# Theta's products in float32 on the transposed x, and x in DRAM by pairs of batches

## The chip, the cores and the metric

The kernel runs on one NeuronCore of a Trainium2 chip. Its engines are TensorE (PE in the profile, PEld for its weight loads), VectorE (DVE), ScalarE (ACT), GpSimd (POOL) and SyncE (SP, which issues the DMAs). The metric is the device time of one execution in microseconds (us).

## The reference

Three layers run one after the other on B = 4 batches of S = 768 positions with DM = 320 channels (8 heads of 40). The first is a gated linear attention; its output, laid out as x[b, s, 320], feeds the second layer, which is the one that the change touches:

```
theta = x @ w_theta
zr = x * cos(theta);  zi = x * sin(theta)
y = einsum('ts,bsd->btd', w_tok_r, zr) + einsum('ts,bsd->btd', w_tok_i, zi)
u = x + y
x2 = u + max(u @ w_ch, 0)
```

The third layer takes x2: a convolution of 5 taps over positions with a sigmoid gives a gate, and the output is (gate * (x2 @ w_val)) @ w_out. All of it is float32.

## The kernel before

The program is written as a list of steps, and a planner sets the order. Each call on `pe`, `act`, `dve`, `pool`, `sp` (or on a choice of two, such as `any2`, DVE or POOL) is recorded by `Unit.record` (line 67 of the profile is that helper, so nearly all instructions carry L67). `Plan.order` then runs a list schedule: each step has a cost from `Plan.cost`, a due time that comes from PE's order, and the free engine that can take it first gets it; a step with two possible engines gets the slower one only while its due time allows. `Plan.issue` repeats this four times and keeps the order with the earliest planned end. A change to one part can so move instructions everywhere, and move steps between DVE and POOL.

The work has two stages. In the first, `attend(d)` runs attention over 12 groups (a batch and a pair of 128-position chunks each). `finish(g)` scales the group's output in a tile `x_m` (two 640-column multiplications, on DVE or POOL), and `store_x(g)` writes it to the DRAM tile `x_dr`, laid out [batch, position, 320], with two DMAs. Between groups `cv_piece` turns a third of a weight matrix from 64-bit into float32, and for theta's weights into a rounded high part `th_hi` and a low part `th_lo`.

In the second stage `theta(p, c)` runs 12 times, for two pairs of batches p and six chunks c of 128 positions (steps 1 to 6 are p = 0, steps 7 to 12 are p = 1). One step reads x of both batches into a tile `x_m` with two DMAs, transposes it on PE in five blocks of 128 columns (the fifth holds the last 64 channels of both batches), and copies it out of PSUM twice: with ACT into the tile `xT_m`, which is u's place later on, and as a rounded high part and a low part into `xh_m` (ACT copies, DVE subtracts, lines 797 to 807). PE then forms theta for each batch out of eight products of 320 columns: high by high, high by low and low by high for two blocks, and two products for the last block. ACT rounds theta to a whole number of turns (`th_m`), DVE subtracts, ACT takes the sine and cosine, and for both parts x is multiplied in and the result split into high and low (`z`; 640 columns each, on DVE or POOL).

`weight(p, th_i, c)` prepares the token weights of a step: DVE works on the bits of a 64-bit tile (`r_b`) and subtracts to get the low part (`wt_m`); for the second pair they are read back from DRAM (`w_r`). `mix` multiplies z by them, 30 products of 384 columns per step, into five PSUM banks. Between the mixes the functions `f_u`, `f_ch`, `f_val` and `f_out` do the rest of the layers: `f_u` adds the mix's result into `xT_m`, then come products with `ch`, the convolution on DVE, products with `val` and with `out`. Within the planned order every engine works strictly in its own row, and semaphores join them.

Of the kernel before, what the change touches and what calls it, by code (L numbers as in the profile page):

```python
# [7 lines left out]
F32 = mybir.dt.float32  # L8
F32R = mybir.dt.float32r
# [3 lines left out]
AF = mybir.ActivationFunctionType  # L13
ALU = mybir.AluOpType
# [3 lines left out]
B, H, S, D = 4, 8, 768, 40  # L18
DM = H * D
L = 128  # L20
# [52 lines left out]
class Plan:  # L73
# [47 lines left out]
    def cost(self, unit, op, out, ins):  # L121

        n = self.elems(out, 1)
        if unit == "pe":
            if op == "transpose":
                return 0.11
            m, kind = ins[0].shape[-1], ins[0].dtype
            if kind == F32R:
                return (n + 32) / 2400
            rows = 2 if ins[0].shape[0] <= 64 else 1  # L130
            tiles = rows * (2 if m <= 64 else 1)
            if kind == BF16:
                return max((n + 6) / 2400, 0.05) / tiles
            return 2 * max((2 * n + 10) / 2400, (m + 6) / 1200) / tiles
        if unit == "act":
            return n / 1200 + (0.051 if ins[0].space == PSUM else 0.093) + 0.093 * (len(ins) > 1)
        if unit == "pool":
            if op == "tensor_tensor":
                wide = all(st or c == 1 for a in ins for st, c in list(a.ap)[1:])
                return n * (0.0021 if wide else 0.00166) + 0.15  # L140
            return n / 1200 + {"affine_select": 0.2, "tensor_copy": 0.17, "copy": 0.17}.get(op, 0.035)
        if unit == "sp":
            return self.DMA_ISSUE
        fast = op in ("tensor_scalar", "tensor_copy", "copy") and all(a.space != PSUM for a in [out] + ins)
        each = 0.06 * any(self.elems(a, 1) == 1 < n for a in ins)
        return n * (6 if op == "reciprocal" else 1) / (1920 if fast else 960) + 0.068 + each
# [195 lines left out]
def tile_kernel(ctx, tc, qT, kT, kt, v1, og, ig, fg, w_th, w_ch, w_val, w_out, cw, wtok,  # L342
# [17 lines left out]
    def words(n, name, dtype=F32, place=None, bufs=1):  # L360

        t = sb.tile([128, n], dtype, name=name, tag=place or name, bufs=bufs)
        k = turn(place, bufs) if place else 0
        plan.place[t.name] = f"{place or name}.{k}"
        return t
# [3 lines left out]
    halfpi, magic = words(1, "halfpi"), words(1, "magic")  # L369
    dve.memset(halfpi, HALFPI)  # L370
    dve.memset(magic, MAGIC)
    x_dr = dr.tile([B, S, DM], F32, name="x_dr")
    wt_dr = dr.tile([2, NC, 128, 4 * TH], F32, name="wt_dr")


    wsp = {}
    for nm, n, m in (("th", DM, DM), ("ch", 384, 256), ("val", 384, 256), ("out", DM, DM)):
        wsp[nm] = [words(3 * c, f"{nm}_{s}", F32R).rearrange("p (k n) -> p k n", k=3)
                   for s, c in (("hi", n), ("lo", m))]

# [80 lines left out]
    def half(i):  # L461
        return slice(64 * i, 64 * i + 64)
# [134 lines left out]
    def store_x(g):  # L597
        b, g3 = divmod(g, NC // GC)
        so = st.pop(("so", g)).rearrange("p (u d) -> p u d", u=2)
        for i in range(2):  # L600
            t0 = (g3 * GC + i) * L
            sp.dma_start(out=x_dr[b, t0:t0 + L, :].rearrange("(u p) d -> p u d", p=U), in_=so[half(i)])


    def cv_piece(nm, src, k_):
        t = turn("cv", 2)
        raw = xT_m[1][:, t * 2 * DM:(t + 1) * 2 * DM].bitcast(I64)
        v = xT_m[1][:, (4 + t) * DM:(5 + t) * DM]
        if nm == "cw":
            raw, v = raw[:, 0:15], cw_sb.rearrange("p j t -> p (j t)")  # L610
        sp.dma_start(out=raw, in_=src if nm == "cw" else src[:, k_ * DM:(k_ + 1) * DM])
        cv_abs(raw, v)
        cv_bits(raw, v)
        if nm == "cw":
            return
        if nm == "th":
            dve.tensor_scalar(out=v, in0=v, scalar1=INV2PI, scalar2=None, op0=ALU.mult)
        hi, lo = wsp[nm]
        act.activation(out=hi[:, k_, 0:DM], in_=v, func=AF.Copy)
        n = DM if nm in ("th", "out") else 256  # L620
        any2.tensor_tensor(out=lo[:, k_], in0=v[:, 0:n], in1=hi[:, k_, 0:n].bitcast(F32),
                           op=ALU.subtract)
        if n < DM:
            any2.tensor_tensor(out=hi[:, k_, DM:384], in0=v[:, 256:DM],
                               in1=hi[:, k_, 256:DM].bitcast(F32), op=ALU.subtract)
# [126 lines left out]
            store_x(d)  # L752


    xh_m = words(20 * L, "xh_m", F32R, place="xh").rearrange("p (j l) -> p j l", l=L)
    wt_m = [words(4 * TH, f"wt_m{i}", F32R, place=f"w{i}").rearrange("p (s r t) -> p s r t", s=2, r=2)
            for i in range(2)]
    hl_f = words(8 * TH, "hl_f", F32R, place="q").rearrange("p (s j t) -> p s j t", s=2, j=4)
# [7 lines left out]


    def blk(x, j):
        return x[:, j * 128:(j + 1) * 128]

    def passes(out, prods):
        with plan.joined():
            for n, (l, r) in enumerate(prods):
                pe.matmul(out, l, r, start=n == 0, stop=n == len(prods) - 1)

    def split_rest(src, sr, eng):

        act.activation(out=sr[0:64, 0], in_=src[0:64], func=AF.Copy)
        act.activation(out=sr[64:128, 1], in_=src[64:128], func=AF.Copy)
        eng.tensor_tensor(out=sr[64:128, 0], in0=src[0:64], in1=sr[0:64, 0].bitcast(F32),  # L780
                          op=ALU.subtract)
        eng.tensor_tensor(out=sr[0:64, 1], in0=src[64:128], in1=sr[64:128, 1].bitcast(F32),
                          op=ALU.subtract)

    def ps_tile():
        return bank[turn("s", 2)] if stage[0] == 0 else (
# [2 lines left out]

    def theta(p, c):  # L790
        x = x_m[turn("x", XB)]
        src = x_dr[2 * p:2 * p + 2, c * L:(c + 1) * L, :].rearrange("b t d -> t b d")
        sp.dma_start(out=x[:, 0:512].rearrange("t (b d) -> t b d", b=2), in_=src[:, :, 0:256])
        sp.dma_start(out=x[:, 512:640].rearrange("t (b d) -> t b d", b=2), in_=src[:, :, 256:DM])
        xT = st["xT", p, c // 3] = xT_m[c // 3].rearrange("p (j t) -> p j t", j=5)
        o = slice((c % 3) * L, (c % 3) * L + L)
        xm = xh_m[:, 10 * (c % 2):10 * (c % 2 + 1)]
        xh, xl, xr = xm[:, 0:4], xm[:, 4:8], xm[:, 8:10]
        tps = ps_tile().rearrange("p (j l) -> p j l", j=4)
        with plan.joined():  # L800
            for j in range(4):
                pe.transpose(tps[:, j, :], blk(x, j), id_sb)
        tp4 = ps_tile()[:, 0:L]
        pe.transpose(tp4, blk(x, 4), id_sb)
        act.activation(out=xh, in_=tps, func=AF.Copy)
        dve.tensor_tensor(out=xl, in0=tps, in1=xh.bitcast(F32), op=ALU.subtract)
        split_rest(tp4, xr, dve)
        act.activation(out=xT[:, 0:4, o], in_=tps, func=AF.Copy)
        act.activation(out=xT[:, 4, o], in_=tp4, func=AF.Copy)
        wh, wl = wsp["th"]  # L810
        fr, rn = th_m[:, 0:2 * DM], th_m[:, 2 * DM:3 * DM]
        sc = th_m[:, 3 * DM:7 * DM].rearrange("p (r d) -> p r d", r=2)
        for bb in range(2):
            th = ps_tile()[:, 0:DM]
            pr = []
            for k_ in range(2):
                j = 2 * bb + k_
                pr += [(xh[:, j], wh[:, k_]), (xh[:, j], wl[:, k_]), (xl[:, j], wh[:, k_])]
            passes(th, pr + [(xr[:, bb], wh[:, 2]), (xr[:, bb], wl[:, 2])])

            act.activation(out=rn, in_=th, func=AF.Identity, bias=magic)
            for a, n, o in ((0, 256, 256 * bb), (256, 64, 512 + 64 * bb)):
                dve.scalar_tensor_tensor(out=fr[:, o:o + n], in0=rn[:, a:a + n], scalar=MAGIC,
                                         in1=th[:, a:a + n], op0=ALU.subtract, op1=ALU.subtract)
        z_hi, z_lo = (words(4 * DM, "z", F32R, place="z", bufs=2 * NC)
                      .rearrange("p (r d) -> p r d", r=2) for _ in range(2))
        with plan.joined():
            act.activation(out=sc[:, 1], in_=fr, func=AF.Sin, scale=-TWOPI)
            act.activation(out=fr, in_=fr, func=AF.Abs)
            act.activation(out=sc[:, 0], in_=fr, func=AF.Sin, scale=-TWOPI, bias=halfpi)  # L830
        for ri in (1, 0):
            any2.tensor_tensor(out=sc[:, ri], in0=sc[:, ri], in1=x, op=ALU.mult)
            act.activation(out=z_hi[:, ri], in_=sc[:, ri], func=AF.Copy)
            any2.tensor_tensor(out=z_lo[:, ri], in0=sc[:, ri], in1=z_hi[:, ri].bitcast(F32),
                               op=ALU.subtract)
        st["z", p, c] = (z_hi, z_lo)
# [289 lines left out]
```

## Time and profile before

| | |
|---|---|
| time, median of 3 runs | 427.25 us (426.7 to 428.12) |
| the profiled execution's own time | 428.13 us |
| its span, first to last instruction | 426.4 us |
| mean granted clock of TensorE | 0.872 of full speed |
| attention | up to about 125 us |
| theta steps 1 to 6, first mixes | 125 to 208 us |
| first fused part (`f_u` to `f_val`) beside mixes | 208 to 250 us |
| theta steps 7 to 12 beside mixes, `out`, `ch` | 250 to 322 us |
| the rest | 322 to 426.4 us |

The profile comes from one execution. Its span is 1.7 us shorter than that execution's time, since the start and the end of the program lie outside it. Busy time of an engine is the time in which at least one of its instructions runs; instructions of one engine overlap a little, so the mean of one instruction is somewhat longer than the distance between two. A row of the timeline ends with the idle time of the engine just before it and with what ended that idle time.

### The profile page before, as it was taken

How to read it: one execution, taken by the hardware profiler on the slowest of the kernel's cores; microseconds unless marked ns; L12 is line 12 of the kernel's file. 1: busy time of each engine (PE TensorE's matmuls, PEld its weight loads, DVE VectorE, ACT ScalarE, POOL GpSimd, SP SyncE). 2: the span in 40 equal slices, each digit the busy share in tenths (PEclk: the TensorE clock that was granted, in tenths of full speed). 3: DMA queues.
4: the chain of work that ended last, by engine and by line, in shares of the span. 5: the costliest groups of instructions: out<-in, count | busy, mean ns of one | idle time of the engine just before them, and what ended most of it. 6: DMA issues, size and time to landing. Idle time of an engine off the chain costs nothing.

```text
span 426.4 us, 11793 instructions
## 1 busy us (share of the span) xinstructions
PE 369.0 (87%) x4876; PEld 348.0 (82%) x4876; DVE 341.8 (80%) x714; ACT 224.6 (53%) x393; POOL 92.4 (22%) x103
## 2 busy tenths in 40 slices
PE   5686994896977595898999969999999999999985
PEld 4575884786876484798899959999999999999974
DVE  7875788499788689899999996758998449667993
ACT  2660515335126987777545366766578324134634
POOL 1212436142345333200011032005100002011600
PEclk9577568568587579889999989999999999999999
DMA  6986769768787553955856128620221530000202
GB/s 179 248 237 168 229 185 233 209 206 237 219 230 220 168 189 106 302 191 180 317 174 234 47 85 277 234 90 34 74 82 67 180 118 20 0 2 1 78 15 92
DMA packets 32373, 65.64 MB, mean 154 GB/s; under 512 B 6752, under 2 KB 19200, under 8 KB 32320
## 3 DMA queue, kind: packets, MB, share of 16 engines
q1 hardware_dynamic: 32320, 64.90, 48.9%
q8 instruction: 38, 0.62, 0.7%
q14 instruction: 15, 0.12, 0.1%
HBM read 47.58 MB, written 17.30 MB: 152 GB/s over the span
## 4 chain that ended last, share of the span: by engine, by line
PE 50%; DVE 30%; issue 8%; ACT 8%; DMA 2%; SPq 1%; ACTq 0%; DVEq 0%
PE bank L67 50%; DVE k_m L67 10%; DVE th_m L67 3%; DVE r_b L67 3%; DVE z L67 2%; DVE xh_m L67 2%; ACT th_m L67 2%; DVE xT_m L67 1%; ACT xT_m L67 1%; SPq L67 1%; DMA r_b<-in_kt_dram 1%; DVE f_m L67 1%; DMA r_b<-in_wtok_dram 1%; ACT xh_m L67 1%; DVE wt_m L67 1%
## 5 line engine op out<-in xcount | busy, mean ns | idle before, releaser
L67 PE MATMUL bank<-wt_m,z 128*128 128x384 f32 x480 | 88.6, 341 | 2.1 <-DVE th_m L67 1.0
L67 PEld LDWEIGHTS bank<-wt_m,z 128*128 128x128 f32 x480 | 84.5, 191 | 3.0 <-ACT z L67 1.7
L67 DVE SCALAR_TENSOR_TENSOR k_m<-k_m,cw_sb,k_m 128x384 f32<-128x384 f32 x76 | 46.4, 660 | 0.3
L67 PE MATMUL bank<-th_hi,xh_m 128*128 128x320 f32 x120 | 34.8, 364 | 12.4 <-DVE xh_m L67 7.9
L67 PE MATMUL bank<-w_r,z 128*128 128x384 f32 x240 | 43.7, 337 | 0.0
L67 PEld LDWEIGHTS bank<-w_r,z 128*128 128x128 f32 x240 | 41.5, 188 | 0.0
L67 ACT ACTIVATE W<-bank 128x512 f32<-128x512 f32 x24 | 14.2, 596 | 46.4 <-PE bank L67 45.6
L67 PEld LDWEIGHTS bank<-th_hi,xh_m 128*128 128x128 f32 x120 | 24.8, 227 | 15.1 <-DVE xh_m L67 9.3
L67 PE MATMUL bank<-q_m,k_m 40*64 40x64 f32 x768 | 21.2, 274 | 12.7 <-issue 8.4
L67 PEld LDWEIGHTS bank<-q_m,k_m 40*64 40x64 f32 x768 | 19.0, 185 | 13.5 <-issue 9.0
L67 ACT ACT_TABLE_LOAD x19 | 24.4, 1283 | 1.9 <-DVE W L67 1.6
L67 DVE TENSOR_TENSOR W<-W,bank 128x512 f32<-128x512 f32 x24 | 15.5, 676 | 12.3 <-PE bank L67 12.2
L67 PE MATMUL bank<-th_lo,xh_m 128*128 128x320 f32 x72 | 24.9, 347 | 0.0
L67 DVE SCALAR_TENSOR_TENSOR r_b<-r_b,r_b 128x768 int32<-128x768 int32 x24 | 23.9, 999 | 0.2
L67 DVE TENSOR_TENSOR k_m<-k_m,bank 104x164 f32<-104x164 f32 (+1 forms) x36 | 14.9, 421 | 10.1 <-PE bank L67 7.0
L67 PE MATMUL bank<-r_b,kw_m 64*40 64x41 f32 x704 | 19.1, 250 | 3.8 <-issue 2.5
L67 ACT ACTIVATE f_m<-bank 64x384 f32<-64x384 f32 x16 | 7.8, 486 | 27.3 <-PE bank L67 26.0
L67 PE MATMUL bank<-r_b,W 64*64 64x41 f32 x768 | 20.4, 272 | 1.4 <-issue 1.4
L67 ACT ACTIVATE th_m<-th_m 128x640 f32<-128x640 f32 (+1 forms) x27 | 18.9, 702 | 5.0 <-DVE th_m L67 3.1
L67 DVE TENSOR_TENSOR xh_m<-bank,xh_m 64x128 fp32r<-64x128 f32 (+1 forms) x36 | 15.2, 422 | 7.3 <-ACT xT_m L67 4.8
L67 PEld LDWEIGHTS bank<-r_b,W 64*64 64x64 f32 x768 | 18.5, 184 | 2.9 <-issue 2.8
L67 PEld LDWEIGHTS bank<-r_b,kw_m 64*40 64x40 f32 x704 | 15.9, 159 | 6.0 <-issue 3.1
(172 smaller groups left out, 936.3 us busy)
## 6 DMA issues: line engine op xcount, KB each, us to landing
r_b<-in_wtok_dram SPq DMA_DIRECT2D x24, 384.0 KB
wt_dr<-wt_m SPq DMA_DIRECT2D x12, 768.0 KB
w_r<-wt_dr SPq DMA_DIRECT2D x8, 768.0 KB
r_b<-in_v_dram SPq DMA_DIRECT2D x12, 328.0 KB
q_m<-in_qT_dram SPq DMA_DIRECT2D x24, 160.0 KB
k_m<-in_kT_dram SPq DMA_DIRECT2D x24, 160.0 KB
r_b<-in_kt_dram SPq DMA_DIRECT2D x12, 320.0 KB
x_m<-in_og_dram SPq DMA_DIRECT2D x24, 160.0 KB
```

Source lines behind the costliest of these rows:

```text
L67: calls[u] = lambda e=e: getattr(e, op)(*args, **kw)
```

## The change

Theta's weights are no longer split. `cv_piece` scales the float32 weights into a tile `w_t[0]`, and ACT copies them into a second one, `w_t[1]`, whose columns are in another order (the last 64 first). Theta's products take the transposed x in `xT_m` and these weights as float32: three products per batch, two with 128 rows and one with the 64 rows of the last block. `xh_m`, its copies and subtractions and the helper `split_rest` are gone. In DRAM x now lies by pairs of batches: [pair, position, 640], the first batch's 320 channels, then the second batch's last 64, then its first 256. So the middle 128 columns are the block that both batches share, a step reads x with one DMA, and the rounded theta is subtracted with one instruction of 320 columns instead of two. `store_x` needs two DMAs for each half of an odd batch. In `Plan.cost` a wide float32 product no longer counts as sharing the array.

```diff
@@ Plan.cost
             tiles = rows * (2 if m <= 64 else 1)
+            if kind == F32 and n > U:
+                tiles = 1
@@ tiles
-    x_dr = dr.tile([B, S, DM], F32, name="x_dr")
+    x_dr = dr.tile([B // 2, S, 2 * DM], F32, name="x_dr")
+    w_t = [words(3 * DM, f"w_t{bb}").rearrange("p (k n) -> p k n", k=3) for bb in range(2)]
-    for nm, n, m in (("th", DM, DM), ("ch", 384, 256), ("val", 384, 256), ("out", DM, DM)):
+    for nm, n, m in (("ch", 384, 256), ("val", 384, 256), ("out", DM, DM)):
@@ store_x
-            sp.dma_start(out=x_dr[b, t0:t0 + L, :].rearrange("(u p) d -> p u d", p=U), in_=so[half(i)])
+            to = x_dr[b // 2, t0:t0 + L].rearrange("(u p) d -> p u d", p=U)
+            if b % 2 == 0:
+                sp.dma_start(out=to[:, :, 0:DM], in_=so[half(i)])
+            else:
+                sp.dma_start(out=to[:, :, 384:], in_=so[half(i), :, 0:256])
+                sp.dma_start(out=to[:, :, DM:384], in_=so[half(i), :, 256:DM])
@@ cv_piece
         if nm == "th":
-            dve.tensor_scalar(out=v, in0=v, scalar1=INV2PI, scalar2=None, op0=ALU.mult)
+            w0, w1 = (t[:, k_] for t in w_t)
+            dve.tensor_scalar(out=w0, in0=v, scalar1=INV2PI, scalar2=None, op0=ALU.mult)
+            act.activation(out=w1[:, 64:], in_=w0[:, 0:256], func=AF.Copy)
+            act.activation(out=w1[:, 0:64], in_=w0[:, 256:], func=AF.Copy)
+            return
@@ blk
-        return x[:, j * 128:(j + 1) * 128]
+        o = (0, 1, 3, 4, 2)[j] * 128
+        return x[:, o:o + 128]
@@ theta
-        src = x_dr[2 * p:2 * p + 2, c * L:(c + 1) * L, :].rearrange("b t d -> t b d")
-        sp.dma_start(out=x[:, 0:512].rearrange("t (b d) -> t b d", b=2), in_=src[:, :, 0:256])
-        sp.dma_start(out=x[:, 512:640].rearrange("t (b d) -> t b d", b=2), in_=src[:, :, 256:DM])
+        sp.dma_start(out=x, in_=x_dr[p, c * L:(c + 1) * L])
...
-        act.activation(out=xh, in_=tps, func=AF.Copy)
-        dve.tensor_tensor(out=xl, in0=tps, in1=xh.bitcast(F32), op=ALU.subtract)
-        split_rest(tp4, xr, dve)
         act.activation(out=xT[:, 0:4, o], in_=tps, func=AF.Copy)
         act.activation(out=xT[:, 4, o], in_=tp4, func=AF.Copy)
...
-                pr += [(xh[:, j], wh[:, k_]), (xh[:, j], wl[:, k_]), (xl[:, j], wh[:, k_])]
-            passes(th, pr + [(xr[:, bb], wh[:, 2]), (xr[:, bb], wl[:, 2])])
+            r = slice(64 * bb, 64 * bb + 64)
+            passes(th, [(xT[:, 2 * bb + k_, o], w_t[bb][:, k_]) for k_ in range(2)]
+                   + [(xT[r, 4, o], w_t[bb][r, 2])])
             act.activation(out=rn, in_=th, func=AF.Identity, bias=magic)
-            for a, n, o in ((0, 256, 256 * bb), (256, 64, 512 + 64 * bb)):
-                dve.scalar_tensor_tensor(out=fr[:, o:o + n], in0=rn[:, a:a + n], scalar=MAGIC,
-                                         in1=th[:, a:a + n], op0=ALU.subtract, op1=ALU.subtract)
+            dve.scalar_tensor_tensor(out=fr[:, bb * DM:(bb + 1) * DM], in0=rn, scalar=MAGIC, in1=th,
+                                     op0=ALU.subtract, op1=ALU.subtract)
```

The planner makes a new order out of this, for all engines. Counted over the whole program, DVE has 716 instructions before and 675 now, ACT 395 and 361, POOL 108 and 86; SP has 240 of them both times. Two places of the order follow; in it `bank_106` and the like are PSUM banks, a name with a number is one of several equal tiles, and "x3" is a row that repeats.

On PE, behind the last products with `val` of the first fused part, where step 7 begins, there stood before:

```order
L67 MATMUL bank_108<-sr_f,val_hi 128x384
L67 MATMUL bank_106<-id_sb,x_m_82 128x128 x4
L67 MATMUL bank_107<-id_sb,x_m_82 128x128
L67 MATMUL bank_108<-th_hi,xh_m 128x320
L67 MATMUL bank_108<-th_lo,xh_m 128x320
L67 MATMUL bank_108<-th_hi,xh_m 128x320 x2
L67 MATMUL bank_108<-th_lo,xh_m 128x320
```

and there stands now (`id_sb` with `x_m` are the transposes, `wt_m` with `z` the mix):

```order
L67 MATMUL bank_108<-sr_f,val_hi 128x384
L67 MATMUL bank_106<-id_sb,x_m_82 128x128 x4
L67 MATMUL bank_107<-id_sb,x_m_82 128x128
L67 MATMUL bank_101<-wt_m_109,z 128x384 x6
L67 MATMUL bank_108<-w_t_71,xT_m_90 128x320 x3
L67 MATMUL bank_106<-w_t_72,xT_m_90 128x320 x3
L67 MATMUL bank_102<-wt_m_109,z 128x384 x6
```

The first six of the 30 products of a mix moved in between the transposes and theta's products, of which there are six in place of sixteen.

On POOL, at the end of attention and in theta steps 1 to 6, there stood before (`x_m` by `num_m` is attention's last scaling, `z` and `th_m` are theta's):

```order
L67 MEMSET k_m_87 128x5x4
L67 TENSOR_TENSOR z<-th_m,z 128x640 x2
L67 TENSOR_TENSOR x_m_79<-x_m_79,num_m 128x640
L67 TENSOR_TENSOR val_lo<-xT_m_91,val_hi 128x256
L67 TENSOR_TENSOR val_hi<-xT_m_91,val_hi 128x64
L67 TENSOR_TENSOR out_lo<-xT_m_91,out_hi 128x320
L67 TENSOR_TENSOR x_m_80<-x_m_80,num_m 128x640
L67 TENSOR_TENSOR th_m<-th_m,x_m_82 128x640
```

and there stands now:

```order
L67 MEMSET k_m_87 128x5x4
L67 TENSOR_TENSOR wt_m_109<-r_b_86,wt_m_109 128x768
L67 TENSOR_TENSOR val_lo<-xT_m_91,val_hi 128x256 x2
L67 TENSOR_TENSOR hl_f<-xT_m_90,hl_f 128x768
L67 TENSOR_TENSOR hl_f<-k_m_87,hl_f 128x768
L67 COPY halo<-k_m_87 128x20
```

The `z`, `th_m` and `x_m` instructions of this stretch are in DVE's row now; in the whole program POOL keeps two of theta's 640-column instructions (eight before) and three of attention's (eight before).

## Rows read from the trace of the kernel before

**Rows 1.** The page: busy time, share of the span and instructions by engine.

```profile
PE 369.0 (87%) x4876; PEld 348.0 (82%) x4876; DVE 341.8 (80%) x714; ACT 224.6 (53%) x393; POOL 92.4 (22%) x103
```

**Rows 2.** Windows: start:end, length, busy by engine (instructions), clock, DMA share, GB/s.

```profile
125.00:208.00 83.00, 65.24 (x637) 59.94 (x637) 72.67 (x148) 61.85 (x106) 18.34 (x15) 0.84 0.63 201
208.00:250.00 42.00, 40.51 (x235) 39.97 (x233) 41.06 (x72) 20.07 (x29) 5.72 (x4) 1.00 0.44 161
250.00:322.00 72.00, 68.75 (x412) 67.44 (x412) 59.08 (x112) 49.40 (x92) 12.71 (x8) 0.98 0.42 140
```

**Rows 3.** Chain that ended last: start us, length us, what it ran through.

```profile
252.84 38.75 PE bank L67 x231
...
322.16 67.27 PE bank L67 x393
```

**Rows 4.** Groups: count, busy us, mean ns, idle before; last row: ns min/median/max, first and last start.

```profile
L67 DVE TENSOR_TENSOR xh_m<-bank,xh_m 64x128 fp32r<-64x128 f32 (+1 forms) x36 | 15.2, 422 | 7.3 <-ACT xT_m L67 4.8 <-ACT xh_m L67 1.9
...
L67 ACT ACTIVATE xh_m<-bank 64x128 fp32r<-64x128 f32 (+1 forms) x36 | 12.2, 373 | 5.6 <-DVE num_m L67 4.7 <-PE bank L67 0.7
...
L67 DVE SCALAR_TENSOR_TENSOR th_m<-th_m,bank 128x256 f32<-128x256 f32 x24 | 10.0, 418 | 1.9 <-ACT th_m L67 1.5
...
L67 DVE SCALAR_TENSOR_TENSOR th_m<-th_m,bank 128x64 f32<-128x64 f32 x24 | 5.1, 214 | 0.0
...
L67 DVE SCALAR_TENSOR_TENSOR th_m<-th_m,bank x48: 209/314/422, 134.5 to 320.0; 128x256 f32<-128x256 f32 x24, 128x64 f32<-128x64 f32 x24
```

**Rows 5.** Groups: 640-column instructions of theta and attention, by engine.

```profile
L67 DVE TENSOR_TENSOR z<-th_m,z 128x640 fp32r<-128x640 f32 x21 | 16.6, 818 | 0.1
...
L67 POOL TENSOR_TENSOR x_m<-x_m,num_m 128x640 f32<-128x640 f32 x8 | 11.2, 1397 | 14.2 <-DVE num_m L67 4.3 <-DVE x_m L67 3.7 <-DMA k_m<-in_selG_dram 3.5
...
L67 POOL TENSOR_TENSOR th_m<-th_m,x_m 128x640 f32<-128x640 f32 x5 | 8.4, 1678 | 23.9 <-ACT th_m L67 23.9
...
L67 POOL TENSOR_TENSOR z<-th_m,z 128x640 fp32r<-128x640 f32 x3 | 5.2, 1755 | 18.6 <-ACT z L67 18.6
```

**Rows 6.** Timeline of DVE: first and last of five waits for x parts behind 134.5.

```profile
149.57 1.33 DVE L67 TENSOR_TENSOR xh_m<-bank,xh_m 128x512 fp32r<-128x512 f32 x3 [0.42 <-ACT xT_m L67]
...
194.05 1.01 DVE L67 TENSOR_TENSOR xh_m<-bank,xh_m 128x512 fp32r<-128x512 f32 x2 [0.80 <-ACT xT_m L67]
```

**Rows 7.** Timeline of PE: eight products of step 3, the transposes behind, warm-up; its window.

```profile
158.23 0.32 PE L67 MATMUL bank<-th_hi,xh_m 128*128 128x320 f32 x1
...
159.41 0.71 PE L67 MATMUL bank<-id_sb,x_m 128*128 128x128 f32 x5
...
2.08 5.68 PE L67 MATMUL bank<-num_m 128*128 128x256 f32 x14 [2.08 <-DVE halfpi L67]
...
4.00:6.00 2.00, 2.00 (x6) 1.64 (x5) 1.97 (x6) 0.00 (x0) 0.29 (x1) 1.00 0.53 161
```

**Rows 8.** Timeline of PE at step 7: transposes, first products, the rest, the mix.

```profile
247.80 0.71 PE L67 MATMUL bank<-id_sb,x_m 128*128 128x128 f32 x5
250.13 0.38 PE L67 MATMUL bank<-th_hi,xh_m 128*128 128x320 f32 x1 [1.62 <-DVE f_m L67]
...
252.84 0.90 PE L67 MATMUL bank<-th_hi,xh_m 128*128 128x320 f32 x2 [2.18 <-DVE xh_m L67]
...
256.47 5.37 PE L67 MATMUL bank<-wt_m,z 128*128 128x384 f32 x30
```

**Rows 9.** Waits, first and second half: who for whom, us, times, longest.

```profile
PE bank L67 <- DVE xh_m L67: 5.1, 4, 1.7
...
PE bank L67 <- DVE xh_m L67: 2.8, 2, 2.2
```

**Rows 10.** DMAs of x on SP (ns, first and last start), transposes of step 1.

```profile
L67 SPq DMA_DIRECT2D x_dr<-x_m x24: 575/602/1971, 43.5 to 170.0; - x24
L67 SPq DMA_DIRECT2D x_m<-x_dr x24: 365/422/597, 117.4 to 265.1; - x24
...
127.09 1.33 PE L67 MATMUL bank<-id_sb,x_m 128*128 128x128 f32 x5
```

More of the change, by code (lines that the diff above doesn't have):

```diff
@@ L616, in cv_piece @@
         if nm == "th":
-            dve.tensor_scalar(out=v, in0=v, scalar1=INV2PI, scalar2=None, op0=ALU.mult)
+            w0, w1 = (t[:, k_] for t in w_t)
[3 more added lines that the diff above has]
+            return
         hi, lo = wsp[nm]
         act.activation(out=hi[:, k_, 0:DM], in_=v, func=AF.Copy)
-        n = DM if nm in ("th", "out") else 256
+        n = DM if nm == "out" else 256
         any2.tensor_tensor(out=lo[:, k_], in0=v[:, 0:n], in1=hi[:, k_, 0:n].bitcast(F32),
@@ L752, in attend @@
             store_x(d)
-    xh_m = words(20 * L, "xh_m", F32R, place="xh").rearrange("p (j l) -> p j l", l=L)
     wt_m = [words(4 * TH, f"wt_m{i}", F32R, place=f"w{i}").rearrange("p (s r t) -> p s r t", s=2, r=2)
@@ L774, in passes @@
                 pe.matmul(out, l, r, start=n == 0, stop=n == len(prods) - 1)
[L776 to L783, printed above, removed]
     def ps_tile():
@@ L791, in theta @@
         x = x_m[turn("x", XB)]
-        src = x_dr[2 * p:2 * p + 2, c * L:(c + 1) * L, :].rearrange("b t d -> t b d")
-        sp.dma_start(out=x[:, 0:512].rearrange("t (b d) -> t b d", b=2), in_=src[:, :, 0:256])
-        sp.dma_start(out=x[:, 512:640].rearrange("t (b d) -> t b d", b=2), in_=src[:, :, 256:DM])
+        sp.dma_start(out=x, in_=x_dr[p, c * L:(c + 1) * L])
         xT = st["xT", p, c // 3] = xT_m[c // 3].rearrange("p (j t) -> p j t", j=5)
         o = slice((c % 3) * L, (c % 3) * L + L)
-        xm = xh_m[:, 10 * (c % 2):10 * (c % 2 + 1)]
-        xh, xl, xr = xm[:, 0:4], xm[:, 4:8], xm[:, 8:10]
         tps = ps_tile().rearrange("p (j l) -> p j l", j=4)
@@ L804, in theta @@
         pe.transpose(tp4, blk(x, 4), id_sb)
-        act.activation(out=xh, in_=tps, func=AF.Copy)
-        dve.tensor_tensor(out=xl, in0=tps, in1=xh.bitcast(F32), op=ALU.subtract)
-        split_rest(tp4, xr, dve)
         act.activation(out=xT[:, 0:4, o], in_=tps, func=AF.Copy)
         act.activation(out=xT[:, 4, o], in_=tp4, func=AF.Copy)
-        wh, wl = wsp["th"]
         fr, rn = th_m[:, 0:2 * DM], th_m[:, 2 * DM:3 * DM]
@@ L814, in theta @@
             th = ps_tile()[:, 0:DM]
-            pr = []
-            for k_ in range(2):
-                j = 2 * bb + k_
-                pr += [(xh[:, j], wh[:, k_]), (xh[:, j], wl[:, k_]), (xl[:, j], wh[:, k_])]
-            passes(th, pr + [(xr[:, bb], wh[:, 2]), (xr[:, bb], wl[:, 2])])
+            r = slice(64 * bb, 64 * bb + 64)
+            passes(th, [(xT[:, 2 * bb + k_, o], w_t[bb][:, k_]) for k_ in range(2)]
+                   + [(xT[r, 4, o], w_t[bb][r, 2])])
             act.activation(out=rn, in_=th, func=AF.Identity, bias=magic)
-            for a, n, o in ((0, 256, 256 * bb), (256, 64, 512 + 64 * bb)):
-                dve.scalar_tensor_tensor(out=fr[:, o:o + n], in0=rn[:, a:a + n], scalar=MAGIC,
-                                         in1=th[:, a:a + n], op0=ALU.subtract, op1=ALU.subtract)
+            dve.scalar_tensor_tensor(out=fr[:, bb * DM:(bb + 1) * DM], in0=rn, scalar=MAGIC, in1=th,
+                                     op0=ALU.subtract, op1=ALU.subtract)
         z_hi, z_lo = (words(4 * DM, "z", F32R, place="z", bufs=2 * NC)
```

## Prediction

> **What bounds the kernel now.** The page's busy line comes first [rows 1]: PE 87%, DVE 80%, ACT 53%, POOL 22%. Two engines near their limit say little before the span is cut in stages, so the busy time by windows is read next [rows 2]. Attention fills the time up to about 125 us; the change leaves its work alone but for its stores and three small weight pieces. From 125 to 208 us, where theta steps 1 to 6 lie, PE is busy 65.2 of 83 us and DVE 72.7: DVE is the fuller engine, with some 10 us idle. From 208 to 250 us (no theta there) DVE is busy 41.1 of 42 us. From 250 to 322 us, where steps 7 to 12 lie, PE is busy 68.8 of 72 us and DVE 59.1: there PE sets the pace. The chain of waits says the same: from 252.84 us it runs through PE alone for 38.75 us and from 322.16 us, behind the last step, through PE for 67.27 [rows 3]. So the change has to be priced twice, in the first half in DVE time and in the second in PE time. What moves ahead of 322 us moves the end by as much, since the order of the work behind it stays the same.
>
> **What a theta step saves on DVE and ACT.** DVE loses three subtractions of x's parts per step (36 at a mean of 0.422 us [rows 4], 1.27 us a step). Its four subtractions from PSUM (two of 256 columns at 0.418, two of 64 at 0.214: 1.26 us) become two of 320. On the line through 64 and 256 columns one of 320 takes 0.486 us, so 0.97: 0.29 us less. That is 1.56 us a step, 18.7 over twelve. ACT loses three copies a step (36 at 0.373 us, 1.12 a step); at 53% busy this counts only where PE or DVE waits for ACT.
>
> **DVE does not keep that gain.** The new plan hands work back from POOL to DVE: of theta's 640-column multiplications and subtractions POOL did eight and now does two, of attention's last scalings eight and now three [rows 5]. Between the first theta subtraction (134.5 us [rows 4]) and 250 us that is three `z`, one `th_m` and two `x_m` instructions on DVE at 0.82 us each: 4.9 us. Taken away in the same stretch are the x parts of five steps (5 x 1.27 = 6.3 us; step 1's lie before it) and twelve PSUM pairs become shorter (12 x 0.146 = 1.7 us). The small weight subtractions that DVE gains and one for `hl_f` that POOL gains are taken to cancel. Sum: -6.3 - 1.7 + 4.9 = -3.1 us, not the 8 that the diff suggests. DVE also waits five times for its next x parts, 0.42, 0.53, 0.26, 1.56 and 0.80 us, 3.6 in all [rows 6]. Those waits go, but I let the longer product put as much back, because DVE's next theta subtraction needs that product. **First half: -3.1 us**; ends 0 (the product's latency eats the gain as well) and -6.7 (none of the 3.6 us comes back).
>
> **The products on PE.** A step has 16 products of 320 columns with rounded operands. At the upper clock level (2.4 GHz) eight of them take 1.18 us, from 158.23 to 159.41 [rows 7]: 0.1475 us each, 2.36 a step. Now it has six float32 products of two instructions each. No row shows one of 320 columns. The nearest is the warm-up at 2.08 us: seven products of 256 columns, 14 instructions in 5.68 us, 0.406 us each [rows 7]. If that ran at the lower level (1.2 GHz), it compares with the 14 rounded products from 252.84 to 256.47 us [rows 8], 0.259 us for 320 columns and 0.207 for 256: an instruction is 1.96 passes, and a step takes 12 x 1.96 x 0.1475 = 3.47 us, 1.11 more than now. If it ran at the 1.00 that the window shows for it, an instruction is 0.406 / 0.118 = 3.4 passes and a step takes 6.0 us, 3.7 more. I take the first: 1.96 is nearly a whole number of passes, and where PE starts after another long idle, as at 252.84 us, its products are spaced for the lower level.
>
> The Trainium skill has a rule for this choice, in "FP8 and Floating Point Precision", TensorE Precision Notes: a true FP32 product goes through the array four times. By that rule a step would take an estimated 24 x 0.1475 = 3.54 us; the window's 1.00 contradicts it, the spacing at the lower level agrees.
>
> **Second half, in PE time.** Six steps at +1.11 us are +6.7 us. Against this stands the entry. PE transposes for step 7 at 247.80 us and is done 0.7 us later; it waits 1.62 us for a PSUM bank that DVE empties, issues two products, waits 2.18 us for DVE's x parts, and the other 14 products take 3.63 us instead of 14 x 0.1475 = 2.07, since the clock has dropped [rows 8]. After the change nothing of step 7 on DVE stands between transposes and products, and six products of the mix come first on PE. Of the 3.80 us of waits I leave 0.9 (those six need a weight tile that DVE writes): -2.9 us. The clock's loss of 1.6 us goes too if PE idles no longer than that. The rest of the 2.8 us of waits for x parts in this half [rows 9] is -0.6 us. Sum: 6.7 - 2.9 - 1.6 - 0.6 = **+1.6 us**; ends -1 (all 3.8 us of waits go, and DVE's lighter load lets later mixes start sooner) and +8.3 (nothing is given back, and step 7's longer products run at the lower level: 6.7 + 1.6).
>
> **Edits at nothing.** The store of x for odd batches becomes two issues (12 more at a median of 0.602 us on SP's queue), the reads halve (12 fewer at 0.422) [rows 10]: +2.2 us of issuing over 125 us in which SP mostly waits. What hides it: the first read of x is issued at 117.4 us and its transposes start at 127.09. Without that cover step 1 would be late by the issues ahead of it, at most 12 x 0.6 = 7 us. The weight pieces of theta lose a subtraction and gain two short copies on ACT, long before their use. The products of steps 7 to 12 now read the transposed tile of the first pair's place; the copies that fill it waited for that place before, so no wait is new.
>
> **Sum.** -3.1 + 1.6 = -1.5 us. The profiled execution took 428.13 us (span 426.4 and 1.73 around it) and would take 426.6; it lay 0.9 us above the median of 427.25, from which the forecast counts: 425.7 us.
>
> **The rivals.**
> - *PE pays in full* (slower). Step 7 keeps its waits in another form: PE idles for the weight tile of the six products ahead, drops a level, and six steps of +1.11 us stand without refund: +8.3 us. With the first half's -3.1 that is +5.2, without it +8.3: 432.5 to 435.5. It decides at step 7: if its products start later than they do now (250.13 us, less what the first half gained), the refund is gone. For it: DVE is 98% busy just there. Against: the two waits in rows 8 name a PSUM bank and x parts, and the second goes.
> - *Nothing moves.* The halves cancel within 1.3 us, because DVE's gain goes to each product's longer latency: 427.25.
> - *DVE was the brake on PE* (faster). PE waits 5.1 us for x parts in the first half [rows 9]; if mixes run in those gaps and DVE's waits go as well, the first half gives -6.7 and the second +0.5: 421.
> - *The float32 product is the dear one*, 3.4 passes: six steps at +3.7 us in the second half, less the entry's 5, and nothing from the first: 444.
>
> **How the numbers follow.** Chances: forecast 0.42 (own range 423 to 428), PE pays in full 0.25, nothing moves 0.16, the brake 0.14, the dear product 0.03. The range of 420.5 to 432.5 leaves out the dear product, most of "PE pays" beyond its first price and the lower end of the brake, about 2 in 10. A measurement here can tell 0.3%, 1.3 us, from no change, so faster means below 426.0. The forecast gives 0.27 to faster, 0.12 to the middle and 0.03 to slower; the brake 0.14 to faster; "nothing moves" 0.15 to the middle and 0.01 to faster; the other two 0.28 to slower. Faster 0.42, same 0.27, slower 0.31.
>
> **What would show it.** A 320-column float32 instruction should be spaced 0.29 us at the upper level; 0.5 would mean the dear product. POOL's busy time falls by some 15 us and DVE's by 4 to 6. The first addition into `xT_m` (208 us now) comes up to 3 us sooner, and step 7's first product before 249 us, with the clock at 1.00. From there to the last theta step the stretch grows by 1 to 2 us. If PE waits over 2 us on DVE ahead of step 7, or DVE's idle time up to 208 us does not shrink, the forecast is wrong and the slower rival is right.

## The result, and the profile after

| | before | after |
|---|---|---|
| median of 16 runs each | 428.14 us (425.48 to 434.16) | 422.44 us (419.63 to 428.01) |
| ratio after to before, 95% interval | | 0.9874 (0.9846 to 0.9903) |
| the same pair in a later set (17 and 12 runs) | 427.56 us | 427.25 us, ratio 1.0021 (0.9984 to 1.0059) |

The change made the kernel 5.4 us faster in the first set of runs (the ratio times 428.14), and made no difference in the second. The medians are over all runs, the ratios leave out executions that took over 1.5% longer than the fastest of the same kernel, so the two differ a little. The intervals of the two sets don't meet, so an interval from one set leaves out something that differs between sets; where that lies comes below. The kernel before took 427.6 to 429.3 us in the four sets on record; it is the changed kernel that moved. The forecast was -1.5 us.

The profile of after comes from an execution of 426.55 us, above the median; a second profile of the same kernel, of 427.25 us, agrees with it to 0.5 us in every stretch. Its busy line, and the windows that answer to [rows 1] and [rows 2]:

```profile
PE 376.9 (89%) x4828; PEld 334.2 (79%) x4828; DVE 330.5 (78%) x673; ACT 212.6 (50%) x359; POOL 66.6 (16%) x81
```

```profile
125.00:208.00 83.00, 74.82 (x685) 58.71 (x678) 77.85 (x145) 58.37 (x93) 10.38 (x10) 0.93 0.72 234
208.00:250.00 42.00, 40.86 (x225) 38.14 (x224) 40.75 (x69) 19.18 (x30) 4.92 (x3) 1.00 0.38 143
250.00:322.00 72.00, 72.00 (x377) 61.52 (x376) 46.81 (x81) 45.79 (x75) 6.02 (x4) 1.00 0.34 116
```

In the first window PE is busy 74.8 us where it was 65.2, in the third it is busy all the time. Over the program POOL is busy 26 us less and DVE 11 us less; the prediction had some 15 and 4 to 6. The chain of waits (start, length, what it ran through) shows the same in one row: in place of the two rows [rows 3] PE runs without a gap that matters from step 7 to the last mix.

```profile
244.28 143.21 PE bank L67 x780
```

Fixed windows cut the two programs at different work, so the comparison that counts is by stretches of the same work. **Stretch 1** goes from the first theta subtraction on DVE to the first addition into `xT_m`, **stretch 2** from there to the last product of the last mix. Before, then after (start:end, length, busy PE, PEld, DVE, ACT, POOL, clock, DMA share, GB/s):

```profile
134.51:208.25 73.74, 57.32 (x483) 52.91 (x484) 65.33 (x130) 57.96 (x98) 16.53 (x14) 0.86 0.60 197
208.25:389.42 181.17, 176.26 (x1039) 174.42 (x1038) 144.72 (x261) 95.83 (x164) 26.30 (x18) 0.99 0.32 111
```

```profile
133.26:203.28 70.02, 61.84 (x487) 47.59 (x486) 66.64 (x118) 52.84 (x84) 5.43 (x7) 0.95 0.69 230
203.28:387.47 184.19, 183.05 (x1011) 169.84 (x1010) 135.27 (x232) 90.42 (x145) 19.71 (x14) 1.00 0.29 103
```

Stretch 1 became 3.7 us shorter and stretch 2 became 3.0 us longer. Read PE's column as work and idle time: 16.4 us of idle time in stretch 1 became 8.2, 4.9 in stretch 2 became 1.1, together 12.0 us less; PE's busy time grew by 4.5 and 6.8, together 11.3. So the change took idle time from PE and filled nearly all of it with its own longer products. What lies behind stretch 2 is the same work in both, 37.0 and 37.3 us.

Stretch 1 begins at the first theta subtraction of step 1, so what the change saves in step 1 itself lies ahead of it. Before, step 1's transposes start at 127.09 us [rows 10] and its first theta subtraction at

```profile
134.51 0.54 DVE L67 SCALAR_TENSOR_TENSOR th_m<-th_m,bank 128x256 f32<-128x256 f32 x2
```

In the second profile of after the two stand at

```profile
128.80 1.33 PE L67 MATMUL bank<-id_sb,x_m 128*128 128x128 f32 x5
```

```profile
133.70 0.48 DVE L67 SCALAR_TENSOR_TENSOR th_m<-th_m,bank 128x320 f32<-128x320 f32 x1
```

So 7.4 us became 4.9: the copies and subtractions of x's parts no longer stand between transposes and products. From step 1's first transpose to the end of the span is 299.3 us before and 296.3 and 296.7 in the two profiles of after, 2.6 to 3.0 us less. That much of the gain repeats; the rest of the first set's 5.4 us lies ahead of that transpose.

Step 7, which answers to [rows 8], on PE of after (start, length, instruction; behind it the idle time and what ended it):

```profile
244.28 1.14 PE L67 MATMUL bank<-wt_m,z 128*128 128x384 f32 x5 [1.07 <-DVE wt_m L67]
245.25 3.98 PE L67 MATMUL bank<-w_t,xT_m 128*128 128x320 f32 x12
249.16 3.04 PE L67 MATMUL bank<-wt_m,z 128*128 128x384 f32 x16
```

One wait of 1.07 us for the weight tile is left of the 3.80 us, the clock stays at 1.00, and from the start of the twelve float32 instructions to the start of what follows is 3.91 us: 0.326 us each, 1.55 us a step more than the 2.36 of before.

The 640-column instructions of theta and attention, which answer to [rows 5] (count, busy us, mean ns, idle before): POOL keeps two `th_m` and three `x_m`; the rest is DVE's.

```profile
L67 DVE TENSOR_TENSOR z<-th_m,z 128x640 fp32r<-128x640 f32 x24 | 19.1, 818 | 0.7 <-ACT z L67 0.6
L67 DVE TENSOR_TENSOR th_m<-th_m,x_m 128x640 f32<-128x640 f32 x22 | 17.4, 819 | 1.6 <-ACT th_m L67 1.6
L67 DVE TENSOR_TENSOR x_m<-x_m,num_m 128x640 f32<-128x640 f32 x21 | 17.2, 819 | 0.1
...
L67 POOL TENSOR_TENSOR x_m<-x_m,num_m 128x640 f32<-128x640 f32 x3 | 3.8, 1262 | 4.0 <-DVE num_m L67 2.9 <-issue 1.1
...
L67 POOL TENSOR_TENSOR th_m<-th_m,x_m 128x640 f32<-128x640 f32 x2 | 3.1, 1572 | 40.5 <-ACT th_m L67 40.5
```

### The profile page after: what moved, and what is told of

It reads as the page before. It is cut to its first block, busy times and chain, and to the rows that moved or that the text cites. A ratio compares the mean times of both kernels' runs of the same rounds, so it can differ in the third digit from the quotient of the medians.

```text
span 424.8 us, 11565 instructions
## 1 busy us (share of the span) xinstructions
PE 376.9 (89%) x4828; PEld 334.2 (79%) x4828; DVE 330.5 (78%) x673; ACT 212.6 (50%) x359; POOL 66.6 (16%) x81
## 4 chain that ended last, share of the span: by engine, by line
PE 54%; DVE 17%; issue 5%; ACT 4%; DMA 1%; POOL 0%; DVEq 0%; ACTq 0%; SPq 0%
PE bank L67 54%; DVE k_m L67 8%; DVE r_b L67 2%; DVE xT_m L67 1%; ACT th_m L67 1%; DMA xT_m<-in_w_out_dram 1%; DVE hl_z L67 1%; DVE num_m L67 1%; ACT L67 1%; DVE th_m L67 1%; DVE wt_m L67 1%; DVE z L67 1%; ACT xT_m L67 1%; DVE f_m L67 1%; ACT hl_z L67 0%
## 5 line engine op out<-in xcount | busy, mean ns | idle before, releaser
L67 PEld LDWEIGHTS bank<-wt_m,z 128*128 128x128 f32 x480 | 82.7, 188 | 7.8 <-issue 3.5
L67 PE MATMUL bank<-w_t,xT_m 128*128 128x320 f32 x144 | 48.7, 464 | 2.3 <-ACT xT_m L67 2.3
L67 DVE SCALAR_TENSOR_TENSOR k_m<-k_m,cw_sb,k_m 128x384 f32<-128x384 f32 x76 | 44.8, 642 | 0.4
L67 PEld LDWEIGHTS bank<-w_t,xT_m 128*128 128x128 f32 x144 | 24.1, 190 | 23.0 <-issue 13.8
L67 PE MATMUL bank<-q_m,k_m 40*64 40x64 f32 x768 | 19.7, 263 | 9.8 <-issue 6.9
L67 PE MATMUL bank<-k_m,q_m 40*64 40x41 f32 x384 | 18.2, 275 | 7.0 <-issue 7.0
L67 ACT ACTIVATE th_m<-bank,magic 128x320 f32<-128x320 f32 x24 | 12.6, 525 | 22.9 <-PE bank L67 19.1
L67 PEld LDWEIGHTS bank<-k_m,q_m 40*64 40x64 f32 x384 | 15.3, 187 | 7.5 <-POOL kw_m L67 3.9
L67 ACT ACTIVATE z<-th_m 128x640 fp32r<-128x640 f32 x24 | 17.3, 733 | 6.9 <-DVE th_m L67 6.9
L67 PE MATMUL bank<-r_b,kw_m 64*40 64x41 f32 x704 | 17.1, 236 | 4.1 <-issue 2.8
```

What stands on the lines that cost most here:

```text
L67: calls[u] = lambda e=e: getattr(e, op)(*args, **kw)
```

## The experiments

All stretches are read from the windows of each kernel's own profile, as above; PE's share is written as busy + idle, and "both" is the sum of the two stretches. "Step 1" is the time from its first transpose on PE to the first theta subtraction, which lies ahead of stretch 1.

| kernel | step 1 | stretch 1 (PE) | stretch 2 (PE) | both |
|---|---|---|---|---|
| before | 7.4 | 73.7 (57.3 + 16.4) | 181.2 (176.3 + 4.9) | 254.9 |
| after | 4.8 | 70.0 (61.8 + 8.2) | 184.2 (183.1 + 1.1) | 254.2 |
| after, second profile | 4.9 | 70.3 (62.0 + 8.3) | 184.2 (183.0 + 1.2) | 254.5 |
| layout alone | 7.1 | 74.4 (59.7 + 14.7) | 180.8 (176.2 + 4.6) | 255.2 |
| float32 alone | 5.1 | 67.2 (60.4 + 6.8) | 186.4 (183.8 + 2.6) | 253.6 |
| old work, new order | 7.0 | 81.2 (63.2 + 18.0) | 185.6 (178.0 + 7.7) | 266.9 |
| new work, old order | 5.7 | 68.8 (60.4 + 8.3) | 185.9 (184.1 + 1.8) | 254.7 |
| more DVE work in steps 1 to 6 | 4.8 | 73.7 (64.2 + 9.5) | 183.9 (182.7 + 1.2) | 257.5 |
| more PE work in steps 7 to 12 | 5.4 | 70.2 (63.4 + 6.8) | 196.2 (195.1 + 1.2) | 266.5 |
| float32 in steps 1 to 6 only | 4.6 | 71.5 (64.7 + 6.8) | 179.4 (174.8 + 4.6) | 250.9 |

The step-1 time falls in every kernel that forms step 1's theta in float32 (4.6 to 5.7 us) and in none that keeps the rounded products there (7.0 to 7.4), in either order.

Two theories were set against each other first: that the gain is work taken away, and that it is a luckier order.

### 1. Each edit alone

The layout alone is the kernel before with the diff's edits to `x_dr`, `store_x`, the read and `blk`, and

```diff
-            for a, n, o in ((0, 256, 256 * bb), (256, 64, 512 + 64 * bb)):
+            for a, n, o in ((0, DM, 0),) if bb == 0 else ((0, 256, 384), (256, 64, DM)):
```

> The kernel before with the second edit alone: x in DRAM by pairs of batches, one read and one or two stores, theta's products still rounded; the subtraction from PSUM is one of 320 columns for the first batch and two (256 and 64) for the second. The planner makes its own order. Work theory (the gain is work taken off DVE): DVE loses 6 x 0.146 us ahead of 208 us, so 427 to 428, ratio 0.998 to 1.000. Order theory (the gain is a luckier order): anything from 0.985 to 1.01, and not tied to DVE's busy time.

Measured: 429.04 us, ratio 1.0025 (0.9984 to 1.0066); both stretches together 0.3 us longer. So nothing is seen of the layout and its 12 more DMA issues for stores, either way.

Float32 alone is the changed kernel with `x_dr`, `store_x`, the read, `blk` and the four subtractions as they were, and one copy of `w_t`.

> The first edit alone: theta's products in float32 on the transposed x, x in DRAM by batches as before (two reads a step, four subtractions from PSUM a step). The planner makes its own order. Work theory: all but the 1.7 us of shorter PSUM subtractions ahead of 250 us, so 423.5 to 425, ratio 0.989 to 0.993. Order theory: 0.985 to 1.01, not tied to DVE's busy time.

Measured: 426.26 us, ratio 0.9935 (0.9887 to 0.9983), just outside the 0.989 to 0.993 that the work theory gave. So the float32 products carry the change; without the layout stretch 1 is even shorter and stretch 2 longer.

### 2. Work and order crossed

The planner plans one kernel, and the other kernel's calls are issued in the places of its steps: `plan.replace` empties a step but leaves its cost, and `plan.silent` adds a call that the planner doesn't see. The core of old work in new order, cut at the dots (`pr` holds the other six products):

```diff
             passes(th, [(xT[:, 2 * bb + k_, o], w_t[bb][:, k_]) for k_ in range(2)]
                    + [(xT[r, 4, o], w_t[bb][r, 2])])
+            plan.replace()
...
+            for n, (l, r) in enumerate(pr + [(sr[:, bb], wh[:, 2]), (sr[:, bb], wl[:, 2])]):
+                plan.silent("pe", "matmul", th, l, r, start=n == 0, stop=n == 7)
```

> The work of before (rounded products, x's high and low parts, two subtractions for the second batch) put into the order of the changed kernel: the planner still plans float32 products, and the rounded ones with their ACT copies and DVE subtractions are issued in their places. Order theory: the order is what helps, so 422 to 424.5, ratio 0.985 to 0.991. Work theory: DVE has its 1.27 us a step back and POOL's work too (4.9 us up to 250 us), so slower than before, 429 to 433, ratio 1.003 to 1.013.

> The work of the changed kernel (float32 products, no x parts, x by pairs, one subtraction of 320 columns a batch) put into the order of before: what is gone is left out of its place, POOL keeps its eight z and th_m and eight x_m instructions. In steps 4 and 10 ACT makes an extra copy of the transposed x for the products, since the place of xT_m is still in use there. Work theory: DVE has 8 us less up to 250 us and gives nothing to it, so 420 to 423, ratio 0.982 to 0.988. Order theory: within 1.5 us of before, ratio 0.997 to 1.003.

Measured: old work in new order 439.77 us, ratio 1.0284 (1.0217 to 1.0352); new work in old order 427.65 us, 0.9966 (0.9919 to 1.0012). The order theory falls: the old work in places planned for the new is 12 us longer in the two stretches. The work theory falls as well as it was put: the new work in the old order was to give 0.982 to 0.988 and gave about what the order theory said of it, and in the trace it gives no more than the change itself. The rows of stretches 1 and 2, old work in new order and then new work in old order:

```profile
136.29:217.50 81.21, 63.24 (x512) 55.85 (x512) 73.59 (x138) 58.32 (x99) 5.83 (x7) 0.86 0.58 189
217.50:403.14 185.64, 177.96 (x1029) 172.69 (x1028) 145.00 (x256) 95.72 (x163) 19.38 (x14) 0.99 0.30 104
```

```profile
128.56:197.31 68.75, 60.43 (x468) 47.07 (x467) 62.04 (x103) 53.58 (x85) 14.14 (x14) 0.93 0.66 228
197.31:383.22 185.91, 184.13 (x1015) 170.36 (x1014) 139.36 (x231) 89.93 (x148) 27.00 (x18) 1.00 0.31 107
```

In the old order POOL keeps its `z`, `th_m` and `x_m` (14.1 us busy), DVE has 4.6 us less to do than after (62.0 to 66.6), and stretch 1 is 1.3 us shorter than after, not 4.6. Then stretch 2 is 1.7 us longer: PE has no idle time left to give there, so that work which stretch 1 leaves over is paid in full (PE has 468 instructions in stretch 1 where after has 487). The three kernels that form theta in float32 in every step, with no load added, come to 253.6 to 254.7 us in four profiles, whatever their order.

### 3. Work added on one engine

The changed kernel and its order, with instructions repeated that give the same result (`plan.twice` issues a step's calls twice; the planner doesn't count them). Behind the subtraction of 320 columns:

```diff
+            if p == 0:
+                plan.twice()
```

and, in the other kernel, behind the three float32 products:

```diff
+            if p == 1 and bb in (0,):
+                plan.twice()
```

> The changed kernel and its order; in steps 1 to 6 each subtraction of 320 columns from PSUM is made twice on DVE (12 more at 0.486 us, 5.8 us in all, the same result). If DVE sets the pace of the first half, as the forecast's sum took it: 5 to 6 us slower, near 428. If PE or the chain of one step does: 0 to 2 us slower.

> The changed kernel and its order; in steps 7 to 12 the three products of the first batch are made twice (six more instructions a step, the same result). At 0.326 us each, as the profile of the changed kernel spaces them, that is 1.95 us a step, 11.7 in all. If PE sets the pace of the second half: 11 to 12 us slower, near 434 where the changed kernel takes 422.4. If something else sets it (DVE's gates, as in steps 1 to 6): less than 6 us.

Measured: 431.13 us with the DVE work, ratio 1.0012 (0.9975 to 1.0049), and 440.47 us with the PE work, ratio 1.0120 (1.0068 to 1.0172), where the kernel before took 428.44 on the same chip. By the ratios that is some 429 and 434 us, as expected if the changed kernel takes 422.4. But no run of the changed kernel stood beside them, and the two sets above show why that matters; the stretches are the safer measure. Stretch 1 with the DVE work, stretch 2 with the PE work:

```profile
128.09:201.77 73.68, 64.20 (x490) 49.76 (x488) 71.56 (x130) 53.10 (x84) 5.28 (x7) 0.93 0.66 216
```

```profile
206.25:402.48 196.23, 195.07 (x1047) 175.63 (x1046) 135.54 (x232) 90.42 (x145) 18.97 (x14) 1.00 0.28 97
```

The 12 instructions more on DVE (5.8 us by their durations, 4.9 us more busy time) made stretch 1 3.5 us longer (73.7 against a mean of 70.2): there added DVE work costs some 60 to 70% of its time. The 36 instructions more on PE (18 products) made stretch 2 12.0 us longer, 0.334 us each, with PE idle for 1.2 us as in after: there PE sets the pace, and a float32 instruction costs its whole spacing.

### 4. The first part by many executions

Both kernels were cut behind one step of the plan, and the rest left out (shown for the first addition into `xT_m`; for attention's last exponential it is the last step of its kind):

```diff
-        for n in best[1]:
+        stop = best[1].index(self.last[0])
+        for n in best[1][:stop + 1]:
```

> The kernel before, cut at the first addition into xT_m: everything that its plan puts behind that addition is left out (so no output is written), what stands ahead of it is unchanged. Its time is the length of the first part alone, attention and theta steps 1 to 6, over many executions instead of one profile: 208.8 us in the profile plus 1.7 around it, so 210 to 211.

> The changed kernel, cut at the same addition, the rest left out. First-part theory (the whole gain arises ahead of this addition, as 208.3 against 203.3 us in the two profiles say): 4 to 6 us below the cut kernel before, 205 to 206. Second-half theory (steps 7 to 12 give most, because step 7 finds its products ready and the clock stays up): 1 to 3 us below it, 208 to 209.

> The kernel before, cut at the last exponential of attention (the last W on ACT), the rest of the plan left out, no output written. In its profile this ends at 143.4 us, so 145 to 146 with what lies around the span.

> The changed kernel, cut at the same exponential, the rest left out. If the first part's gain of 6.8 us arises in the theta steps, where the forecast put it: within 1.5 us of the cut kernel before. If attention itself became shorter (its last W ends at 140.4 us in the profile): 3 to 5 us less.

Measured, cut at the first addition into `xT_m`: 215.14 (213.47 to 217.21) and 208.34 us (204.68 to 211.34), 6.8 apart, and the first 4 us above what was expected. The cut kernels don't end equally soon: the addition starts at 211.21 and 205.09 us in spans of 215.4 and 207.3. Before, a DMA is issued at 211.04, and no engine has work behind 212.2; that the end waits for this DMA is inferred.

```profile
211.21 0.55 DVE L67 TENSOR_TENSOR xT_m<-xT_m,bank 128x384 f32<-128x384 f32 x1 [0.19 <-PE bank L67]
```

```profile
211.04 0.34 SPq L67 DMA_DIRECT2D r_b<-in_wtok_dram  x1
```

```profile
205.09 0.55 DVE L67 TENSOR_TENSOR xT_m<-xT_m,bank 128x384 f32<-128x384 f32 x1
```

Without that difference in what runs behind (4.2 us against 2.2) the first part is some 4.8 us shorter after the change. Cut at attention's last exponential: 146.41 (143.82 to 150.28) and 141.91 us (139.6 to 144.43), 4.5 apart. In these two profiles 1.0 us of it is ACT's order between the last two exponentials, 5.56 us apart before and 4.58 after. ACT's timeline, before and then after:

```profile
138.11 0.58 ACT L67 ACTIVATE W<-bank 128x512 f32<-128x512 f32 x1
138.70 1.28 ACT L67 ACT_TABLE_LOAD   x1
140.00 1.50 ACT L67 ACTIVATE th_m<-th_m 128x640 f32<-128x640 f32 x2
141.53 0.83 ACT L67 ACTIVATE th_m<-th_m,halfpi 128x640 f32<-128x640 f32 x1
142.38 1.28 ACT L67 ACT_TABLE_LOAD   x1
143.67 0.60 ACT L67 ACTIVATE W<-bank 128x512 f32<-128x512 f32 x1
```

```profile
136.32 0.60 ACT L67 ACTIVATE W<-bank 128x512 f32<-128x512 f32 x1 [0.26 <-PE bank L67]
136.93 1.28 ACT L67 ACT_TABLE_LOAD   x1
138.23 1.36 ACT L67 ACTIVATE x_m<-x_m 128x640 f32<-128x640 f32 x2
139.61 1.28 ACT L67 ACT_TABLE_LOAD   x1
140.90 0.60 ACT L67 ACTIVATE W<-bank 128x512 f32<-128x512 f32 x1
```

Before, theta's sine, absolute value and cosine stand there, after, two sigmoids of attention. Most of the rest is step 1 once more, for it runs ahead of these exponentials: from its first transpose to the first of the two it is 9.9 to 10.1 us in the three profiles of the kernel before, whole and cut, and 6.8 to 7.6 in six with the changed kernel's instructions. The two together are 4.0 of the 4.5 us. So the 4.5 us fit the second branch of the expectation, but what became shorter is mostly not attention: it is the step of theta that is mixed into its end. Up to the first transpose no gain is shown: it starts at 127.1, 130.6 and 128.0 us before, and at 128.5, 128.8, 129.6, 129.2, 130.7 and 123.3 after.

That start is what varies most, and with it the first theta subtraction. In the changed kernel with the DVE work, the changed kernel, and the one with the PE work, whose instructions are the same up to there, it stands at

```profile
128.09 1.00 DVE L67 SCALAR_TENSOR_TENSOR th_m<-th_m,bank 128x320 f32<-128x320 f32 x2
```

```profile
133.26 0.48 DVE L67 SCALAR_TENSOR_TENSOR th_m<-th_m,bank 128x320 f32<-128x320 f32 x1
```

```profile
136.02 0.49 DVE L67 SCALAR_TENSOR_TENSOR th_m<-th_m,bank 128x320 f32<-128x320 f32 x1 [0.38 <-ACT th_m L67]
```

The same instructions take 128.1 to 136.0 us, 8 us apart, while stretches 1 and 2 of the changed kernel repeat to 0.6 us wherever no load is added. The first and the last of the three ran on the same chip in the same set, so the chip alone doesn't make that difference.

### 5. The same pair again, and each form where it is cheap

> The changed kernel as it is, beside the others of this set, so that all stand against the same chip's runs of the kernel before, and a second profile of it. Ratio 0.985 to 0.990 as measured at first; if part of that was the chip or the clock of the moment, nearer 0.995.

Measured: ratio 1.0021 (0.9984 to 1.0059), as in the table at the top.

The last kernel keeps theta's weights in both forms and takes the rounded products for the second pair of batches (cut at the dots):

```diff
+            if p:
+                wh, wl = th_hl
+                ...
+                passes(th, pr + [(xr[:, bb], wh[:, 2]), (xr[:, bb], wl[:, 2])])
+            else:
                 passes(th, [(xT[:, 2 * bb + k_, o], w_t[bb][:, k_]) for k_ in range(2)]
```

> Float32 products in steps 1 to 6 as changed, rounded products with high and low parts of x in steps 7 to 12 as before (theta's weights kept in both forms, the split ones made out of the float32 ones in places that attention leaves). If the second half is PE's and the first DVE's: steps 7 to 12 get 6 x 1.5 us of PE back and pay some of it in waits for x parts, so 2 to 7 us faster than the changed kernel, 416 to 421. If the second half gains from having no x parts on DVE ahead of the products as much as it pays on PE: the same as the changed kernel within 1.5 us.

Measured: 420.12 us, ratio 0.9817 (0.9765 to 0.9869) to before, with the changed kernel at 427.25 on the same chip. Its two stretches:

```profile
129.82:201.29 71.47, 64.67 (x488) 49.69 (x487) 66.82 (x118) 53.11 (x84) 5.42 (x7) 0.90 0.66 221
201.29:380.68 179.39, 174.78 (x1035) 172.29 (x1034) 144.04 (x251) 95.09 (x163) 26.69 (x19) 1.00 0.29 106
```

Stretch 2 is 4.8 us shorter than after: 8.3 us of PE's busy time are gone, and 3.5 us of idle time came back, 3.0 of it as waits for x parts. Stretch 1 is 1.2 to 1.5 us longer, so both together give 3.3 to 3.6 us; the other half of the 7.1 lies ahead of the first theta subtraction, where this profile is at 129.8 us, within the spread just shown. In this set it beats both kernels; that it would do so by 7 us in another isn't shown.

## Why the prediction was right or wrong

- **Inside the range and on the right side, but the sum fits neither set.** It was too small against the first set (-5.4; 422.44 us is just below the forecast's own 423 to 428) and too large against the second. In the two stretches that it priced, the trace has -0.4 to -0.7 us; the forecast had -1.5.
- **A term put at nothing: step 1.** The forecast counted from the first theta subtraction and set aside the x parts of step 1, since they "lie before it". They stood between its transposes and its products, and without them step 1 reaches that subtraction 2.4 us sooner (a mean of 7.3 us in three profiles before, of 5.0 in six after). From step 1's first transpose to the first addition into `xT_m` it is 80.9 us before (two profiles) and 75.3 after (four): the first half gives -5.6 us, not -3.1.
- **First half from the first theta subtraction on, -3.1 us: the sum held by luck.** Stretch 1 is 3.4 to 3.7 us shorter. The two DVE terms came as forecast: by its rows in stretch 1, x parts and subtractions from PSUM take 8.2 us less, the 640-column instructions 4.8 us more. But DVE's busy time there did not fall, it rose from 65.3 to 66.6 us, because 4.8 us of other work, 3.0 of it on the token weights (`r_b`), now stand ahead of the first addition. What fell is DVE's idle time, from 8.4 to 3.4 us, and the forecast had put that at nothing, 3.6 us of waits gone and as much put back by the longer product. The step that failed is this choice to price the first half in DVE's busy time alone: waits and moved work, both left out, cancel. New work in the old order, where DVE gets nothing back from POOL, shortens stretch 1 by 5.0 us where the forecast's full price would be 8, and the added DVE work cost 60 to 70% of its time.
- **The float32 product, +1.11 us a step: under-sized.** It is 1.55 (0.326 us an instruction, 0.334 by the added ones). The reading of the warm-up as 1.96 passes was the better of the two (3.4 would have been 0.50 us), but one instruction is 2.2 spacings of a rounded product, so a product is 4.4. The Trainium skill's rule in "FP8 and Floating Point Precision", TensorE Precision Notes, of four passes a product would give an estimated 0.295 us an instruction, with a rounded product's spacing as one pass; the rows here give more.
- **Second half, +1.6 us: +3.0.** The products are 9.3 us in place of 6.7. The refund is 6.3 us in place of 5.1 (2.9 + 1.6 + 0.6): step 7's two waits became one of 1.07 us, PE's idle time in the stretch fell by 3.8, and the clock stayed up. The mis-sized term is the product, 2.6 us too cheap over six steps; the refund was foreseen where it lies.
- **Edits at nothing.** The layout alone bears out the 12 more issues. One wait was overlooked: the products of step 4 read `xT_m`, whose second place still holds the weight pieces of attention's end. The chain of waits of after goes through the last of them, and on through DVE's work on it:

```profile
158.44 5.44 DMA xT_m<-in_w_out_dram
```

Step 4's transposes are issued at 160.80 us there and its products at 169.06. What this costs isn't shown: new work in old order gives step 4 its own copy and has a stretch 1 that is 1.3 us shorter, but the `z`, `th_m` and `x_m` that it leaves on POOL are in the same 1.3 us.
- **The rivals.** "PE pays in full" falls with the row of step 7: the products start at 245.25 us, and the refund came. "The dear product" falls with 0.326 us. "DVE was the brake on PE" had the mechanism right for the first half: PE's idle time in stretch 1 halved, DVE's waits went and did not come back, and -5.6 us with step 1 is nearer to its -6.7 than to the forecast's -3.1 (both were counted without step 1). It had +0.5 for the second half, where 3.0 came. "Nothing moves", within 1.3 us because the halves cancel, is what the two stretches and the second set show, for another reason: not a longer latency in the first half, but PE's longer products in the second. With step 1 the profiles say 2.6 to 3.0 us.
- **Open.** Of the 5.4 us of the first set, 2.6 to 3.0 lie behind step 1's first transpose, in the profiles of either set. What made the changed kernel faster by the rest in one set, and took all of it away in the other, lies ahead of that transpose as far as is known: no profile was taken of an execution of the changed kernel near 422 us, and the profiles behind it repeat. Its cause was not found. The change in attention (`x_m` on DVE at 0.82 us, not on POOL at 1.40) was not separated. The granted clock in the time up to the first theta subtraction is 0.71 in the profile that took 136.0 us and 0.72 in the one that took 128.1, so the clock alone doesn't tell these two apart.

## What to carry to other kernels

Price a change of form in the time of the engine that will be the bound after it: when DVE lets go, PE fills its gaps, and a product that is 1.55 us longer a step is paid in full from then on. Where two halves of a program have different bounds, use each form where it is cheap; here that is worth 3.3 to 3.6 us in the trace. Begin a count ahead of the first instruction that the change touches: the 2.4 us of step 1 fell out of the forecast because it began behind them. And measure a pair in more than one set of runs, or compare stretches of the same work: a stage that varies by 8 us on the same instructions can make or hide an effect of 1%.

## What the runs showed of the hardware

A float32 product of 320 columns is two instructions of 0.326 us at the upper clock level, behind each other without gaps; a rounded product of the same width takes 0.1475 us, eight of them 1.18. With the same instructions ahead of it, the first theta subtraction came at 128.1 to 136.0 us in six profiles (both ends on the same chip), while the two stretches behind it, some 254 us, repeated to 0.6 us where no load was added.
